# Setting a guard's limit to zero in a fused attention and gating kernel

## The chip, the cores and the metric

The kernel runs on one core of a Trainium2 chip. A core has five engines that run side by side, each through its own list of instructions in order: PE (TensorE, matrix products), DVE (VectorE), ACT (ScalarE), POOL (GpSimd) and SP (SyncE, which here only issues transfers). They meet through semaphores. PE reads SBUF and writes PSUM, which has eight banks of 128 x 512 fp32; a product is a weight load (PEld in the profile) followed by a matmul that streams up to 512 columns.

The metric is the device time of one execution in microseconds (us), lower is better. The time before is 208.46 us, the median of 2 runs (208.24 and 208.68).

## The reference

The input x has 2048 rows of 512 numbers. Two branches are computed from it and mixed row by row. Branch A is a linear attention with 32 heads of 16 channels:

```
qkv = x @ wqkv                               q, k, v: 32 heads of 16
pq = q @ w_phi[h] ; pk = k @ w_phi[h]
phi(p) = concat(softmax(p), softmax(-p))     over the 16 features of a head
kv = sum over rows of phi_k^T v ; z = sum over rows of phi_k
o  = (phi_q @ kv) / (phi_q . z + 1e-6)
a  = o @ wo
```

Branch B is a gated MLP with 1376 hidden channels, split into two halves of 688:

```
z = gelu(x @ w_in) ; z1, z2 = halves of z ; z2 = layernorm(z2)
g = w_sp @ z2 + b_sp                         w_sp mixes the 2048 rows
b = (z1 * g) @ w_out
out = s * a + (1 - s) * b,  s = sigmoid(x . gate_w)
```

## The kernel before

The rows are cut into 16 tiles of 128. The kernel has these stages, and every engine gets its instructions in the order in which the program is written (a manual schedule), so that an instruction that waits holds up everything behind it on its engine.

1. **Loads and z.** A few products with constants (spin, L195) come first on PE, then for each tile z = x @ w_in (L186), gelu on ACT, layer norm statistics on DVE, and v = x @ wv. w_phi is folded into wq and wk (L311), so that pq and pk each come from four 128 x 512 products (feat_mm, L335).
2. **K with the row mixing.** For each tile, k_proj makes pk in PSUM, ACT takes exp(pk) and exp(-pk) from it (feat_exp, L343) into a slot of 1024 bf16 numbers, and k_norm divides by the sums: a sum over each group of 16 (L364, DVE), a reciprocal (L365, DVE), and the product, half of it on POOL and half on DVE (both L371). kv_acc adds phi_k^T v of eight groups of heads into PSUM banks 3 and 4 (kv_mm, L407). Between these the products of w_sp with z2 run (gg_half, L435).
3. **Q and the output.** For each tile q_proj and q_norm do the same for q; a transposing DMA on SP's queue turns the slot around (L401). q_mm multiplies it with kv (eight products, L473), q_num divides by the denominators (reciprocal L479 and product L481, both DVE) and sends the result through another transposing DMA on SP's queue (L488). out_tile makes ten 512-column products (six L494, four L499), copies the bank to SBUF on ACT (L508) and sends it to DRAM from ACT's queue.

These exponentials have no maximum subtracted. The kernel therefore keeps a **guard**: in each norm, POOL adds the sums and their reciprocals into a tile called worst, which starts at 1.0 (L180, L367). Near the end check_sums takes each partition's largest entry and writes 1 to safeb where it is at most SAFE, otherwise 0 (L456). count_safe adds the 128 entries of safeb on PE (L461), and set_flag writes 1 to flag if the total is below 127.5 (L466). All engines read that flag into a register (L616), and after the output products of tile 13 (out_mm, into bank 5) they branch on it (L620).

- If the flag is 0, the If block finishes tiles 13, 14 and 15: three copies, the output products of the last two tiles, and the stores.
- If the flag is 1, the Else block computes branch A once more for all 16 tiles, in the **general** form, and writes the whole output again. Here feat_exp_max takes the place of feat_exp: for each sign DVE reduces the 512 numbers of a tile to 32 maxima (or minima) from PSUM, DVE subtracts them into an fp32 buffer, and ACT takes the exponential of that buffer. The norm leaves out the addition to worst. The uT tiles of branch B (the rows z1 * g, transposed) are still in SBUF and are used again.

The PSUM banks of the Else block are 2 and 6 for pk in turn, 5 and 7 for pq, 3 and 4 for kv and for q_mm, and 2 and 6 for the output.

Of the kernel before, what the change touches and what calls it, by code (L numbers as in the profile page):

```python
# [22 lines left out]
NT = S // P  # L23
# [10 lines left out]
QW = HW + 4  # L34
WSLOTS = 8
LAG = 3
SAFE = 1e30


@with_exitstack  # L40
def kernel(
# [285 lines left out]
    def e_slot(i):  # L327
        if i == 5:
            flat = xn[:].rearrange("p t d -> p (t d)")
        else:  # L330
            flat = w_in_flat[:, i * 2 * D:(i + 1) * 2 * D]
        return flat.rearrange("p (g a n) -> p g a n", g=NHG, a=2)
# [27 lines left out]
    def norm(e, watch=True):  # L360
        ev = e.rearrange("p g a (h f) -> p (g a h) f", h=4)
        zr = ring2.tile([P, 2, 2 * H], FP32, name="zr")
        zs, rs = zr[:, 0, :], zr[:, 1, :]
        nc.vector.tensor_reduce(out=zs, in_=ev, axis=AX.X, op=ALU.add)  # L364
        nc.vector.reciprocal(out=rs, in_=zs)  # L365
        if watch:
            nc.gpsimd.tensor_tensor(  # L367
                out=worst[:], in0=worst[:], in1=zr[:].rearrange("p a h -> p (a h)"), op=ALU.add
            )
        for eng, sl in ((nc.gpsimd, slice(H, 2 * H)), (nc.vector, slice(0, H))):  # L370
            eng.tensor_tensor(  # L371
                out=ev[:, sl, :], in0=ev[:, sl, :],
                in1=rs[:, sl, None].to_broadcast([P, H, DH]), op=ALU.mult,
            )

    def feat(t, w, b, e, general):
        for dt in range(NDT):
            feat_mm(t, w, b, dt)
        if general:
            feat_exp_max(b, e, t)  # L380
        else:
            feat_exp(b, e)

    def k_proj(t, general=False):
        ek_t[t] = e_slot(t % 4)
        feat(t, wk, KBANK[t % 2], ek_t[t], general)

    def k_norm(t, watch=True):
        norm(ek_t[t], watch)

    def q_proj(t, general=False):
        eq_t[t] = e_slot(4 + t % 2 if t < 4 else (t - 4) % 6)
        feat(t, wq, QBANK[t % 2], eq_t[t], general)
# [3 lines left out]
    def q_norm(t, watch=True):  # L397
        e = eq_t.pop(t)
        norm(e, watch)
        eT = wqkT[:, 2 * (t % 4):2 * (t % 4) + 2, :].rearrange("p a (b n) -> p (a b) n", n=P)  # L400
        nc.sync.dma_start_transpose(out=eT, in_=e.rearrange("p g a n -> p (g a n)"))  # L401
        eT_t[t] = eT
# [3 lines left out]
    def kv_mm(t, g):  # L406
        nc.tensor.matmul(  # L407
            slots[:, g, 0:HW + 1], lhsT=ek_t[t][:, g, :, :].rearrange("p a n -> p (a n)"),
            rhs=vv[:, t, g, 0:HW + 1],
            start=(t == 0 and g % 4 == 0), stop=(t == NT - 1), skip_group_check=True,  # L410
        )

    def kv_acc(t):
        for g in range(NHG):
            kv_mm(t, g)

    def kv_extract():
        nc.vector.tensor_tensor(
            out=kvx[:, :, 0:HW].rearrange("p g (h d) -> p g h d", h=4),
            in0=slots[:, :, 0:HW].rearrange("p g (h d) -> p g h d", h=4),  # L420
            in1=mask4[:, None, :, None].to_broadcast([P, NHG, 4, DH]), op=ALU.mult,
        )
        nc.vector.scalar_tensor_tensor(
            out=kvx[:, :, HW:QW], in0=slots[:, :, HW:HW + 1].to_broadcast([P, NHG, 4]),
            scalar=0.5 * DEN_EPS, in1=mask4[:, None, :].to_broadcast([P, NHG, 4]),
            op0=ALU.add, op1=ALU.mult,
        )
# [26 lines left out]
    def check_sums():  # L454
        nc.vector.tensor_reduce(out=worst1[:, 0:1], in_=worst[:], axis=AX.X, op=ALU.max)
        nc.vector.tensor_scalar(  # L456
            out=safeb[:], in0=worst1[:, 0:1], scalar1=SAFE, scalar2=None, op0=ALU.is_le
        )
# [13 lines left out]
    def q_mm(t, g):  # L472
        nc.tensor.matmul(  # L473
            slots[:, g, 0:QW], lhsT=eT_t[t][:, g, :], rhs=kvx[:, g, :], start=True, stop=True
        )

    def q_num(t, general=False):
        rd = ring2.tile([P, NHG, 4], FP32, name="rd")
        nc.vector.reciprocal(out=rd[:], in_=slots[:, :, HW:QW])  # L479
        o = ring2.tile([P, D], BF16, name="o")  # L480
        nc.vector.scalar_tensor_tensor(  # L481
            out=o[:].rearrange("p (g h d) -> p g h d", g=NHG, h=4),
            in0=slots[:, :, 0:HW].rearrange("p g (h d) -> p g h d", h=4),
            scalar=gate[:, t:t + 1],
            in1=rd[:, :, :, None].to_broadcast([P, NHG, 4, DH]), op0=ALU.mult, op1=ALU.mult,
        )
        oT = (gTpool if general else oTpool).tile([P, NDT, P], BF16, name="oT")
        nc.sync.dma_start_transpose(out=oT[:, :, :], in_=o[:, :])  # L488
        oT_t[t, general] = oT

    def out_mm(t, b, n0=0, n1=D, general=False):
        uT, oT = uT_t[t], oT_t[t, general]
        for ft in range(NFT):
            nc.tensor.matmul(  # L494
                ps[:, b, n0:n1], lhsT=uT[:, ft, :], rhs=w_out[:, ft, n0:n1],
                start=(ft == 0), stop=False,
            )
        for g in range(NDT):
            nc.tensor.matmul(  # L499
                ps[:, b, n0:n1], lhsT=oT[:, g, :], rhs=wo[:, g, n0:n1],  # L500
                start=False, stop=(g == NDT - 1),
            )

    def out_copy(t, b, ob, copy, dma, n0=0, n1=D):
        if copy is nc.vector:
            nc.vector.tensor_copy(out=ob[:, n0:n1], in_=ps[:, b, n0:n1])  # L506
        else:
            nc.scalar.activation(out=ob[:, n0:n1], in_=ps[:, b, n0:n1], func=AF.Copy)  # L508
        dma.dma_start(out=out2[t * P:(t + 1) * P, n0:n1], in_=ob[:, n0:n1])

    def out_buf():
        return ring3.tile([P, D], BF16, name="ob")

    def out_tile(t, general=False):
        b = (2, 6)[t % 2]
        out_mm(t, b, general=general)
        out_copy(t, b, out_buf(), nc.scalar, nc.scalar)

    uTpool = ctx.enter_context(tc.tile_pool(name="uTp", bufs=NT))
    oTpool = ctx.enter_context(tc.tile_pool(name="oTp", bufs=LAG + 2))  # L520
    gTpool = ctx.enter_context(tc.tile_pool(name="gTp", bufs=2))

    VLAG = 5
    spin(24)
# [95 lines left out]
    with tc.If(unsafe < 1, label="general", preferred_fallthrough_block=False) as branch:  # L620
# [6 lines left out]
        out_mm(NT - 1, 1, D - P, D)  # L627
        out_copy(NT - 1, 1, ob, nc.scalar, nc.scalar, D - P, D)
    with branch.Else():
        for t in range(NT):  # L630
            k_proj(t, general=True)
            k_norm(t, watch=False)
            kv_acc(t)
        kv_extract()
        for t in range(NT):
            q_proj(t, general=True)
            q_norm(t, watch=False)
            for g in range(NHG):
                q_mm(t, g)
            q_num(t, general=True)  # L640
            out_tile(t, general=True)
# [1 line left out]
_INS = ['A_x', 'A_wqkv', 'A_w_phi', 'A_wo', 'B_x', 'B_w_in', 'B_w_sp', 'B_b_sp', 'B_w_out', 'gate_w']  # L643
_OUTS = [((1, 2048, 512), 'bfloat16')]
# [25 lines left out]
```

## Time and profile before

The profile is of one execution that took 208.59 us, 0.13 us above the median. Its span, from the first to the last instruction, is 206.8 us; the remaining 1.8 us lie outside it.

| stretch (us of the span) | what runs | PE busy | DVE busy | ACT busy | POOL busy |
|---|---|---|---|---|---|
| 0 to 62 | z, v, folding | 60.84 | 38.07 | 39.25 | 2.33 |
| 62 to 129 | K with row mixing | 66.58 | 56.26 | 20.13 | 36.26 |
| 129 to 199.5 | Q with output, row mixing | 70.03 | 54.81 | 20.79 | 24.82 |
| 199.5 to 206.8 | the If block | 4.31 | 1.94 | 0.28 | 0.00 |

A row of a group view reads: line, engine, operation, what it writes and reads with shapes, how often; then the busy time in us, the mean duration of one in ns, and how long the engine stood idle before them. A row of a timeline reads: start in us, duration in us, engine (with a q behind it for the issuing of a transfer), line, operation, and how many instructions the row takes together. The end of a matmul is modelled and includes its way through the array, so in a dense stream the distance between the starts of two matmuls is shorter than their durations. The profile gives a granted TensorE clock of 1.000 for every stretch.

### The profile page before, as it was taken

How to read it: one execution, taken by the hardware profiler on the slowest of the kernel's cores; microseconds unless marked ns; L12 is line 12 of the kernel's file. 1: busy time of each engine (PE TensorE's matmuls, PEld its weight loads, DVE VectorE, ACT ScalarE, POOL GpSimd, SP SyncE). 2: the span in 40 equal slices, each digit the busy share in tenths (PEclk: the TensorE clock that was granted, in tenths of full speed). 3: DMA queues.
4: the chain of work that ended last, by engine and by line, in shares of the span. 5: the costliest groups of instructions: out<-in, count | busy, mean ns of one | idle time of the engine just before them, and what ended most of it. 6: DMA issues, size and time to landing. Idle time of an engine off the chain costs nothing.

```text
span 206.8 us, 3753 instructions
## 1 busy us (share of the span) xinstructions
PE 201.8 (98%) x1376; PEld 118.3 (57%) x1400; DVE 151.1 (73%) x310; ACT 80.4 (39%) x142; POOL 63.4 (31%) x79
## 2 busy tenths in 40 slices
PE   8999999999999999999999999999999999999994
PEld 7654555554455666566666667666455554555542
DVE  1077758385887888879897996798989779796512
ACT  4266767675684323250514101222534233241110
POOL 4000000000003464636474755053643363433000
PEclk9999999999999999999999999999999999999999
DMA  6999999998000639473778882135575966777452
GB/s 170 305 164 205 191 172 224 185 188 240 0 3 0 139 66 115 102 141 63 147 124 92 157 172 41 38 82 111 121 152 117 162 132 128 90 162 153 95 120 65
DMA packets 90384, 26.56 MB, mean 128 GB/s; under 512 B 84296, under 2 KB 90360, under 8 KB 90360
## 3 DMA queue, kind: packets, MB, share of 16 engines
q1 hardware_dynamic: 87648, 24.13, 62.0%
q10 hardware_dynamic: 2712, 2.13, 4.0%
q8 instruction: 12, 0.20, 0.4%
q14 instruction: 12, 0.10, 0.2%
HBM read 3.44 MB, written 2.10 MB: 27 GB/s over the span
## 4 chain that ended last, share of the span: by engine, by line
PE 97%; issue 1%; DVE 0%; ACT 0%; DVEq 0%
PE ps L435 36%; PE ps L186 18%; PE ps L335 13%; PE ps L494 10%; PE ps L288 7%; PE ps L499 6%; PE ps L473 2%; PE ps L407 2%; PE ps L195 2%; PE ps L311 1%; PE ps L201 0%; DVE ob L506 0%; ACT ob L508 0%; PE ps L215 0%; PE ps L461 0%
## 5 line engine op out<-in xcount | busy, mean ns | idle before, releaser
L435 PE MATMUL ps<-zz,wsp 128*128 128x344 bf16 x512 | 84.1, 309 | 0.1
L367 POOL TENSOR_TENSOR worst<-worst,zr 128x128 f32<-128x128 f32 x32 | 28.6, 894 | 124.5 <-DVE zr L365 113.8
L435 PEld LDWEIGHTS <-wsp 128*128 128x128 bf16 x512 | 49.8, 98 | 27.9
L343 ACT ACTIVATE w_in<-ps 128x512 bf16<-128x512 f32 x56 | 30.1, 596 | 63.4 <-POOL w_in L371 20.8
L186 PE MATMUL ps<-w_in,xT 128*128 128x512 bf16 (+2 forms) x197 | 40.1, 356 | 0.2
L364 DVE TENSOR_REDUCE zr<-w_in 128x64 f32<-128x1024 bf16 x28 | 33.8, 1208 | 0.0
L443 DVE SCALAR_TENSOR_TENSOR u<-ps,bcol,zz 128x344 bf16<-128x344 f32 x32 | 18.4, 574 | 20.0 <-PE ps L473 8.6
L186 PEld LDWEIGHTS <-xT 128*128 128x128 bf16 x200 | 19.6, 100 | 17.6
L371 POOL TENSOR_TENSOR w_in<-w_in,zr 128x512 bf16<-128x512 bf16 x28 | 29.5, 1052 | 0.0
L221 ACT ACTIVATE zz<-ps 128x1376 bf16<-128x1376 f32 (+2 forms) x18 | 21.4, 1191 | 18.7 <-PE ps L186 18.7
L230 DVE BATCH_NORM_STATS2 stats<-zz 128x6 f32<-128x344 bf16 x32 | 14.9, 507 | 12.9 <-ACT zz L221 12.9
L494 PE MATMUL ps<-w_out,uT 128*128 128x512 bf16 (+2 forms) x100 | 23.4, 366 | 0.2
L407 PE MATMUL ps<-vv,w_in 128*128 128x65 bf16 x128 | 21.7, 193 | 0.0
L371 DVE TENSOR_TENSOR w_in<-w_in,zr 128x512 bf16<-128x512 bf16 x28 | 19.4, 692 | 1.0
L508 ACT ACTIVATE ob<-ps 128x512 bf16<-128x512 f32 (+1 forms) x14 | 8.0, 575 | 27.0 <-PE ps L499 18.2
L365 DVE RECIPROCAL zr<-zr 128x64 f32<-128x64 f32 x32 | 17.7, 553 | 1.1
L335 PEld LDWEIGHTS <-xT 128*128 128x128 bf16 x128 | 10.8, 98 | 9.9
L499 PE MATMUL ps<-wo,oT 128*128 128x512 bf16 (+2 forms) x66 | 16.2, 366 | 0.0
L335 PE MATMUL ps<-wk,xT 128*128 128x512 bf16 x57 | 15.7, 379 | 0.3
L335 PE MATMUL ps<-wq,xT 128*128 128x512 bf16 x57 | 15.6, 379 | 0.3
L473 PE MATMUL ps<-kvx,wqkT 128*128 128x68 bf16 x128 | 15.8, 194 | 0.1
L288 PE MATMUL ps<-wv,xT 128*128 128x512 bf16 x61 | 15.5, 379 | 0.2
(64 smaller groups left out, 145.0 us busy)
## 6 DMA issues: line engine op xcount, KB each, us to landing
out_dram<-ob ACTq DMA_DIRECT2D x13, 128.0 KB, 2.6
w_out<-in_B_w_out_dram SPq DMA_DIRECT2D x1, 640.0 KB, 5.4
w_in<-in_B_w_in_dram SPq DMA_DIRECT2D x2, 256.0 KB, 4.3
wv<-in_A_wqkv_dram SPq DMA_DIRECT2D x1, 512.0 KB, 5.2
wo<-in_A_wo_dram SPq DMA_DIRECT2D x1, 512.0 KB, 5.8
w_in<-in_B_w_in_dram SPq DMA_DIRECT2D x1, 352.0 KB, 4.5
w_in<-in_B_w_in_dram ACTq DMA_DIRECT2D x2, 128.0 KB, 3.9
w_in<-in_B_w_in_dram SPq DMA_DIRECT2D x2, 128.0 KB, 3.5
```

The source lines that it names most:

```text
L186: nc.tensor.matmul(zb[:, n0:n1], lhsT=xT[:, dt, t * P:(t + 1) * P], rhs=w_in[:, dt, n0:n1], start=(dt == 0), stop=(dt == NDT - 1),)
L221: nc.scalar.activation(out=zz[:, t, n0:n1], in_=zbank(t)[:, n0:n1], func=AF.Gelu_apprx_tanh)
L288: nc.tensor.matmul(ps[:, b, :], lhsT=xT[:, dt, t * P:(t + 1) * P], rhs=wv[:, dt, :], start=(dt == 0), stop=(dt == NDT - 1),)
L335: nc.tensor.matmul(ps[:, b, :], lhsT=xT[:, dt, t * P:(t + 1) * P], rhs=w[:, dt, :], start=(dt == 0), stop=(dt == NDT - 1),)
L343: nc.scalar.activation(out=e[:, :, a, :], in_=src, func=AF.Exp, scale=sc)
L364: nc.vector.tensor_reduce(out=zs, in_=ev, axis=AX.X, op=ALU.add)
L367: nc.gpsimd.tensor_tensor(out=worst[:], in0=worst[:], in1=zr[:].rearrange("p a h -> p (a h)"), op=ALU.add)
L371: eng.tensor_tensor(out=ev[:, sl, :], in0=ev[:, sl, :], in1=rs[:, sl, None].to_broadcast([P, H, DH]), op=ALU.mult,)
L407: nc.tensor.matmul(slots[:, g, 0:HW + 1], lhsT=ek_t[t][:, g, :, :].rearrange("p a n -> p (a n)"), rhs=vv[:, t, g, 0:HW + 1], start=(t == 0 ...
L435: nc.tensor.matmul(ps[:, b, 0:HF], lhsT=wsp[:, tt % WSLOTS, s, :], rhs=zz[:, s, FH + h * HF:FH + (h + 1) * HF], start=(s == 0), stop=(s == ...
L494: nc.tensor.matmul(ps[:, b, n0:n1], lhsT=uT[:, ft, :], rhs=w_out[:, ft, n0:n1], start=(ft == 0), stop=False,)
L499: nc.tensor.matmul(ps[:, b, n0:n1], lhsT=oT[:, g, :], rhs=wo[:, g, n0:n1], start=False, stop=(g == NDT - 1),)
```

## The change

SAFE becomes 0.0. Every entry of worst is then compared with 0, so that safeb is 1 only where a partition's largest entry is not above 0. The order of the Else block is rewritten so that tiles overlap: k_proj of tile t+1 is issued ahead of the norm and the accumulation of tile t; q_proj runs two tiles ahead, q_norm one tile ahead, and the output of a tile comes one tile later. The pool of transposed results that only this block uses (gTpool) gets three buffers in place of two. Nothing ahead of the branch is edited but the constant, and the If block stays.

```diff
-SAFE = 1e30
+SAFE = 0.0
...
-    gTpool = ctx.enter_context(tc.tile_pool(name="gTp", bufs=2))
+    gTpool = ctx.enter_context(tc.tile_pool(name="gTp", bufs=3))
...
     with branch.Else():
+        k_proj(0, general=True)
         for t in range(NT):
-            k_proj(t, general=True)
+            if t + 1 < NT:
+                k_proj(t + 1, general=True)
             k_norm(t, watch=False)
             kv_acc(t)
+        q_proj(0, general=True)
+        q_proj(1, general=True)
         kv_extract()
+        q_norm(0, watch=False)
         for t in range(NT):
-            q_proj(t, general=True)
-            q_norm(t, watch=False)
+            if t + 2 < NT:
+                q_proj(t + 2, general=True)
+            if t + 1 < NT:
+                q_norm(t + 1, watch=False)
             for g in range(NHG):
                 q_mm(t, g)
             q_num(t, general=True)
-            out_tile(t, general=True)
+            if t >= 1:
+                out_tile(t - 1, general=True)
+        out_tile(NT - 1, general=True)
```

feat_exp_max, which the Else block calls and the If block never does, reads:

```python
for a, (sc, op) in enumerate(((1.0, ALU.max), (-1.0, ALU.min))):
    nc.vector.tensor_reduce(out=top[:], in_=src, axis=AX.X, op=op)   # PSUM, 512 -> 32
    nc.vector.tensor_tensor(out=d, in0=src, in1=top (broadcast), op=ALU.subtract)
    nc.scalar.activation(out=e[:, :, a, :], in_=d, func=AF.Exp, scale=sc)
```

## The prediction, made before the result was known

> **What bounds the kernel now.** I read the page first (busy time, the 40 slices, the chain), then the groups by line for prices, then the timeline for the distances between instructions, and last the stretch around the branch. From the page:
>
> ```profile
> PE 201.8 (98%) x1376; PEld 118.3 (57%) x1400; DVE 151.1 (73%) x310; ACT 80.4 (39%) x142; POOL 63.4 (31%) x79
> ...
> PE 97%; issue 1%; DVE 0%; ACT 0%; DVEq 0%
> ```
>
> PE is the bound, in every stage: 98% busy and 97% of the chain. DVE, ACT and POOL hide beside it. That is of little use for the changed kernel, since the Else block is work that no row of this trace shows as such. Its prices have to be put together from the groups:
>
> ```profile
> L364 DVE TENSOR_REDUCE zr<-w_in 128x64 f32<-128x1024 bf16 x28 | 33.8, 1208 | 0.0
> L367 POOL TENSOR_TENSOR worst<-worst,zr 128x128 f32<-128x128 f32 x32 | 28.6, 894 | 124.5 <-DVE zr L365 113.8
> L371 POOL TENSOR_TENSOR w_in<-w_in,zr 128x512 bf16<-128x512 bf16 x28 | 29.5, 1052 | 0.0
> ```
>
> A sum over 1024 numbers takes 1.21 us, POOL's half of a norm 1.05 us. DVE's distances from start to start stand in its timeline:
>
> ```profile
> 135.92 0.34 DVE L479 RECIPROCAL rd<-ps 128x32 f32<-128x32 f32 x1
> 136.30 0.75 DVE L481 SCALAR_TENSOR_TENSOR o<-ps,st,rd 128x512 bf16<-128x512 f32 x1
> 136.97 1.21 DVE L364 TENSOR_REDUCE zr<-w_in 128x64 f32<-128x1024 bf16 x1
> 138.21 0.55 DVE L365 RECIPROCAL zr<-zr 128x64 f32<-128x64 f32 x1
> 138.80 0.69 DVE L371 TENSOR_TENSOR w_in<-w_in,zr 128x512 bf16<-128x512 bf16 x1
> 139.41 0.57 DVE L443 SCALAR_TENSOR_TENSOR u<-ps,bcol,zz 128x344 bf16<-128x344 f32 x1
> ```
>
> q_num takes 0.38 + 0.67 = 1.05 us of DVE, a norm 1.24 + 0.59 + 0.61 = 2.44. An instruction that needs the one before it starts 0.03 us after its end, one that doesn't 0.08 before it.
>
> **Which block runs.** worst starts at 1.0 and only gains positive terms, so "at most 0" holds in no partition, the count is 0, and 0 is below 127.5: the flag is 1. The constant itself costs nothing (the comparison stays one instruction of 0.16 us), nor do the third buffer and the new order, unless the Else block runs. Removed is the If block's 7.3 us of span, since PE is done with tile 13 at 199.5; everything ahead of it stays.
>
> **The first general tile.** PE leaves tile 13 at 199.5, four products of 512 columns take 1.03, so DVE's first reduction could start at 200.6. Before, PE goes into the If block without a gap (its first product starts at 199.36), so a branch can be free; the dearest neighbour is SP, which issued its last transfer of L488 1.6 us after what it needed. Bounds 0 and 1.6 us, taken 0.4: **201.0**.
>
> **The new work on DVE.** A reduction of 512: the rows of 1024 (1.208) and of 128 (0.276, L455) give 1.04 ns each and 0.675 for 512, with the 0.03 of a dependent successor 0.71. A subtraction from PSUM: the nearest row is L418, 128x512 from PSUM, 0.680, less 0.08 before an independent successor, 0.61 rounded up. Maxima and minima of a tile: 2 x (0.71 + 0.61) = 2.64 us. Bounds for each of the four: 0.574 (L443, 344 columns) and 0.751 (L481), thus 11 us less or 12 more over 32 tiles. ACT's two exponentials (0.60 each) run beside DVE's next step.
>
> A K tile costs DVE 2.64 + 2.44 = 5.08 us, a Q tile 5.08 + 1.05 = 6.13. PE's K products are only 1.03 + 0.42 us, so PE no longer bounds by its work.
>
> **But PE's order makes DVE wait in K.** On PE, k_proj(t+2) stands behind kv_acc(t), which needs norm(t). DVE's next task after norm(t) is the maximum of t+2. So after each norm, DVE waits for POOL's half, then four of the eight accumulations (those of POOL's half), then four products. POOL's half starts together with DVE's. How late is it? The 128 numbers of worst take POOL 0.89, nearly as long as 512 take alone right after (1.05), and the 0.89 always starts 0.11 after DVE's half, which lasts 0.69. I read this as POOL standing still until DVE's half is over: now POOL's half would end 1.05 after DVE's. Without that wait it would be 0.47 (0.15 + 1.05 - 0.04 - 0.69). I take 1.05.
>
> The Trainium skill (SBUF — State Buffer, section "Who interferes with whom") says that a VectorE instruction with two SBUF inputs and a GpSimd instruction that reads SBUF exclude each other, the later one waiting in full. By it 1.05 holds, without it the sum is 13 us lower; the 0.894 beside 1.052 speaks for it.
>
> **PE's rate.** The granted clock reads 1.000 throughout, yet the trace has two rates:
>
> ```profile
> 0.84 2.72 PE L195 MATMUL ps<-const-bfloat16-1.0 128*128 128x128 bf16 x24 [0.84 <-PEq L654]
> ...
> 20.69 0.39 PE L311 MATMUL ps<-wphi,wqkT 128*128 128x128 bf16 x4
> ```
>
> The same 128 columns are 0.105 us apart at the start ((2.72 - 0.31) / 23), after PE had stood idle, and 0.057 later ((0.39 - 0.22) / 3): a factor of 1.84. The low rate lasted from 0.84 to about 4.6, some 3.8 us of nearly unbroken work. After that PE never rests, so whether a pause brings the low rate back isn't shown. In K, PE would work 1.5 us (2.7 at the low rate) and rest over 5. Such a burst is shorter than the 3.8 us and follows a rest, like the start: I take the low rate in K.
>
> The Trainium skill (TensorE: Matmul & The Clock Gate, "Part 1: The HAM clock gate") states half the clock after an idle window of some 3.4 us, and the full clock again after as long a busy one. The start agrees (3.8 us, 1.84); for the rest no row here does. By it the sum is the 454 below, without it 436.
>
> The wait after a norm is then 1.05 + 0.1 (to PE) + 0.45 (accumulations) + 1.03 x 1.84 = 1.9 + 0.1 (to DVE) = **3.6 us**; at the full rate 1.05 + 0.1 + 0.25 + 1.03 + 0.1 = 2.5. It comes 15 times: ahead of the maxima of tiles 2 to 15 and of the first Q tile. K: 16 x 5.08 + 15 x 3.6 = 135.3, to 336.3.
>
> **Q.** Two maxima, kv_extract (0.68 + 0.18) and norm(0): 5.28 + 0.86 + 2.44 = 8.6, to 344.9. Then the period. DVE alone gives 6.13. A loop over two tiles, from the start of the maximum of t+2: norm(t+1) done at 5.08, POOL and the issue on SP 6.2, the transposing DMA 2.8 (page: 2.7 to 4.9) 9.0, q_mm 9.5, ten output products 11.7, q_proj(t+4), which PE has behind them, 12.8, and DVE starts at 12.9: 6.45 each. SP takes this DMA and that of L488 1.3 apart, so the latter lands near 10.3, before the last four products need it (10.8). At PE's low rate the same loop takes 9.0 + 0.8 + 4.0 + 1.9 + 0.1 = 15.8, or 7.9 each. But here a burst of PE at the low rate lasts 6.7 us, longer than the 3.8 in which the rate rose at the start, and the pauses are near 2.8. I take 6.6, close to the full rate: 13 x 6.6 = 85.8, to 430.7.
>
> **The end.** The last full turn of DVE 6.1, norm(15) 2.44, POOL and issue 1.15, DMA 2.8, q_mm 0.42, q_num 1.15, DMA 2.8, four products 1.03, copy 0.7, store 3.5 (2.6 to land and 0.9 behind it, as at the end before): 22.1, to **452.8**. With the 1.8 us outside the span 454.6; the profiled run is 0.13 above the median, so I say **454 us**.
>
> **Rivals.**
> - PE keeps its full rate. 15 x 1.1 and 13 x 0.15 less: 436 us. The granted clock of 1.000 speaks for it, the first 24 products against it. Chance 0.22.
> - PE is at its low rate in Q too: 13 x 1.3 = 17 more, 471 us. Chance 0.15.
> - DVE never waits, because the products of the next tile are there in time: 15 x 3.6 and 13 x 0.47 less, 394 us. PE's order as written speaks against it. 0.04.
> - The other side, **not slower**: the flag stays 0, the If block runs as before, 208.5 us. It decides at the comparison of L456: one entry of at most 0 as the maximum in all 128 partitions would do, but sums of exponentials and their reciprocals are positive, and worst starts at 1. 0.01.
> - A price above my bounds (fp32 operands on DVE or POOL, a slow fetch of the Else block): over 476. 0.08.
>
> **How the numbers follow.** The forecast has the remaining 0.50; its own range is 440 to 466, from the prices on DVE and from POOL's wait. The range that takes in the neighbours on both sides is 428 to 476; outside lie the last three rivals, 0.13, and the tails of the others. Slower by over 2% 0.99, within 2% 0.01 (2% is about what a measurement of this kernel can tell from no change), faster 0.
>
> **What would show it.** The page after has DVE at some 330 us busy (151 and 180) and PE below 70% of its span, with maxima and subtractions at 64 each near 0.68 us. In K the maximum waits 3.6 us for PE's L335 in every tile, at a period of 8.7; a distance of 0.40 between those four products, not 0.22, shows the low rate. POOL's half starts to last 1.7 where it overlaps DVE's. In Q the period is 6.6. The prediction is wrong if the K period is 7.6 or less, if a subtraction takes 1 us, or if a long gap stands at 199.5.

## The result and the profile after

The changed kernel takes 456.84 us (median of 456.69 and 456.99) against 208.46 before: 2.190 times as long, with a 95% interval of 2.186 to 2.195. The prediction was 454 us in a range of 428 to 476. The profiled execution took 456.99 us, with a span of 455.3.

The page after, lines that answer to those shown of before (busy time of each engine; the granted TensorE clock in 40 slices; the chain of work that ended last; three groups by line, with busy us, mean ns, and idle time before them):

```profile
PE 311.6 (68%) x1914; PEld 159.6 (35%) x1914; DVE 326.7 (72%) x565; ACT 129.7 (28%) x221; POOL 109.9 (24%) x111
...
PEclk9999999999999999995555555555555788779859
...
DVE 9%; PE 8%; DMA 6%; POOL 3%; issue 2%; ACT 0%; POOLq 0%
...
L371 POOL TENSOR_TENSOR w_in<-w_in,zr 128x512 bf16<-128x512 bf16 x56 | 70.3, 1255 | 186.0 <-DVE zr L365 162.3
...
L349 DVE TENSOR_REDUCE top<-ps 128x32 f32<-128x512 f32 x64 | 43.8, 684 | 64.9 <-PE ps L335 64.9
...
L351 DVE TENSOR_TENSOR zz<-ps,top 128x512 f32<-128x512 f32 x64 | 44.3, 692 | 2.2
```

The Else block runs: maxima (L349) and subtractions (L351) are there, 64 of each. The 68 and 72% of the whole span mix two parts: up to 199.5 us PE is busy for 198.4 as before; behind that, in 255.8 us, DVE is busy for 177.7 (69%) and PE for 113.2 (44%), so there no engine is full. The row of L349 says who waits: DVE stood idle for 64.9 us in front of its maxima, all of it for the products of L335. By the timeline 4.0 of these lie in front of the block's first maximum, 46.7 in K (15 waits of 3.12) and 14.2 in Q. PE's granted clock falls to half in the nineteenth of the 40 slices (by the trace's clock records at 206.1 us, 5 us behind PE's first eight products of the block).

Where the 248.5 us of span came from (455.3 less 206.8), read from the starts of L349 in DVE's timeline, beside the prediction's terms:

| stretch | predicted | measured |
|---|---|---|
| first maximum of the Else block at | 201.0 | 200.08 |
| K, to the first maximum of Q | 135.3 | 129.49 |
| into Q, to the maximum of tile 2 | 8.6 | 8.44 |
| 13 Q tiles | 85.8 (6.6 each) | 94.66 (7.28 each) |
| from the maximum of tile 15 to the end | 22.1 | 22.63 |
| span | 452.8 | 455.3 |

K was 5.8 us shorter than forecast and Q 8.9 longer; with the smaller differences in the other rows 2.5 us of the span were left. The two large errors have opposite signs, so the closeness of the total is partly luck.

One K tile of the changed kernel, from the timeline (start, duration, engine, what; in brackets the idle time before it and what ended it):

```profile
211.02 0.69 DVE L349 TENSOR_REDUCE top<-ps 128x32 f32<-128x512 f32 x1 [3.12 <-PE ps L335]
...
215.51 0.69 DVE L371 TENSOR_TENSOR w_in<-w_in,zr 128x512 bf16<-128x512 bf16 x1
215.61 1.51 POOL L371 TENSOR_TENSOR w_in<-w_in,zr 128x512 bf16<-128x512 bf16 x1 [6.79 <-DVE zr L365]
...
217.17 0.40 PE L407 MATMUL ps<-vv,w_in 128*128 128x65 bf16 x4 [0.45 <-POOL w_in L371]
...
217.38 1.90 PE L335 MATMUL ps<-wk,xT 128*128 128x512 bf16 x4
...
219.31 0.69 DVE L349 TENSOR_REDUCE top<-ps 128x32 f32<-128x512 f32 x1 [3.12 <-PE ps L335]
```

DVE's half of the norm ends at 216.20, POOL's at 217.12, then come the four accumulations that need it, then the four products (1.90 us, not the 1.03 they took before), and only at 219.31 DVE's next maximum. The period is 8.29 us, and 3.12 of it are DVE's wait.

### The profile page after: what moved, and what is told of

It is laid out like the page before. It is cut to its first block, busy times and chain, and to the rows that moved or that the text cites. A ratio compares the mean times of both kernels' runs of the same rounds, so it can differ in the third digit from the quotient of the medians.

```text
span 455.3 us, 5445 instructions
## 1 busy us (share of the span) xinstructions
PE 311.6 (68%) x1914; PEld 159.6 (35%) x1914; DVE 326.7 (72%) x565; ACT 129.7 (28%) x221; POOL 109.9 (24%) x111
## 5 line engine op out<-in xcount | busy, mean ns | idle before, releaser
L371 POOL TENSOR_TENSOR w_in<-w_in,zr 128x512 bf16<-128x512 bf16 x56 | 70.3, 1255 | 186.0 <-DVE zr L365 162.3
L349 DVE TENSOR_REDUCE top<-ps 128x32 f32<-128x512 f32 x64 | 43.8, 684 | 64.9 <-PE ps L335 64.9
L355 ACT ACTIVATE w_in<-zz 128x512 bf16<-128x512 f32 x56 | 35.1, 629 | 152.5 <-DVE zz L351 145.9
L364 DVE TENSOR_REDUCE zr<-w_in 128x64 f32<-128x1024 bf16 x56 | 67.7, 1208 | 0.0
L407 PEld LDWEIGHTS <-w_in 128*128 128x128 bf16 x256 | 19.9, 109 | 106.8 <-issue 96.3
L473 PE MATMUL ps<-kvx,wqkT 128*128 128x68 bf16 x256 | 24.5, 209 | 47.0 <-DMA wqkT<-w_in 32.5
L494 PE MATMUL ps<-w_out,uT 128*128 128x512 bf16 x180 | 53.9, 445 | 0.0
L351 DVE TENSOR_TENSOR zz<-ps,top 128x512 f32<-128x512 f32 x64 | 44.3, 692 | 2.2
L335 PE MATMUL ps<-wk,xT 128*128 128x512 bf16 x128 | 44.7, 489 | 0.0
L335 PE MATMUL ps<-wq,xT 128*128 128x512 bf16 x128 | 37.2, 421 | 1.1 <-DVE zz L351 1.1
L473 PEld LDWEIGHTS <-wqkT 128*128 128x128 bf16 x256 | 16.1, 106 | 58.1 <-DMA wqkT<-w_in 40.8
L335 PEld LDWEIGHTS <-xT 128*128 128x128 bf16 x256 | 25.8, 112 | 30.4 <-issue 15.1
L499 PE MATMUL ps<-wo,oT 128*128 128x512 bf16 x120 | 34.8, 417 | 0.3 <-DMA oT<-o 0.3
```

The costliest lines, as they stand in the source:

```text
L335: nc.tensor.matmul(ps[:, b, :], lhsT=xT[:, dt, t * P:(t + 1) * P], rhs=w[:, dt, :], start=(dt == 0), stop=(dt == NDT - 1),)
L349: nc.vector.tensor_reduce(out=top[:], in_=src, axis=AX.X, op=op)
L351: nc.vector.tensor_tensor(out=d.rearrange("p (h f) -> p h f", f=DH), in0=src, in1=top[:, :, None].to_broadcast([P, H, DH]), op=ALU.subtract,)
L371: eng.tensor_tensor(out=ev[:, sl, :], in0=ev[:, sl, :], in1=rs[:, sl, None].to_broadcast([P, H, DH]), op=ALU.mult,)
L407: nc.tensor.matmul(slots[:, g, 0:HW + 1], lhsT=ek_t[t][:, g, :, :].rearrange("p a n -> p (a n)"), rhs=vv[:, t, g, 0:HW + 1], start=(t == 0 ...
L473: nc.tensor.matmul(slots[:, g, 0:QW], lhsT=eT_t[t][:, g, :], rhs=kvx[:, g, :], start=True, stop=True)
```

## The experiments

Times of single executions stand beside 456.84; where there are several, it is said.

### The order alone, and the limit alone

The first kernel is the changed one with the old limit.

```diff
-SAFE = 0.0
+SAFE = 1e30
```

> The new order and the third buffer alone, with the limit back at 1e30. My theory: the Else block isn't entered, and what stands in it costs nothing: 208.5 us, between 207.5 and 209.5. Rival: code that is only fetched or the larger pool costs something of its own: above 212.7.

Measured: 208.41 us (8 runs), 0.9996 times the kernel before, interval 0.996 to 1.003. The new order and the third buffer cost nothing where the Else block isn't entered. The whole slowdown hangs on the constant.

The second is the kernel before with only the constant changed, so that the Else block runs in its old order.

```diff
-SAFE = 1e30
+SAFE = 0.0
```

> The limit at zero alone, with the Else block in its old order. My theory: each Q tile runs through its whole chain by itself (products, maxima, exponentials, norm, transposing DMA, q_mm, q_num, second DMA, output): about 18.6 us a tile; a K tile gains only the 0.8 us in which DVE waits for the exponentials: 9.1 us. Sum 200 + 146 + 298 + 5, about 650 us, between 620 and 680. Rival: the order in which PE takes its work serialises the tiles in the new kernel just as much, so that the old one is within 10% of it: below 503.

Measured: 622.92 us. K takes 9.21 us a tile. Q takes 16.4 and 17.8 in turn, less than the 18.6 expected. They differ because PE's rate rises late in every second tile: the four L499 take 1.04 us in one tile and 1.89 in the tile before. Why both are below 18.6 stays open. Two lines of its timeline show PE in one Q tile, idle until the first transposing DMA has landed and then until the second has:

```profile
493.44 0.63 PE L473 MATMUL ps<-kvx,wqkT 128*128 128x68 bf16 x8 [10.09 <-DMA wqkT<-w_in]
...
497.82 1.04 PE L499 MATMUL ps<-wo,oT 128*128 128x512 bf16 x4 [1.19 <-DMA oT<-o]
```

So the two edits stand against each other in a way that a single comparison with the kernel before can't show: the constant alone adds 414 us, and the new order takes 166 of them back, some 150 of these in Q (K gains 0.92 us a tile).

### Products ahead in K

The products of K tile t+2 go ahead of the accumulation of tile t in PE's order; feat_mm and feat_exp_max are called by themselves for that. DVE's order stays as it was.

```diff
-        k_proj(0, general=True)
+        k_mms(0); k_mms(1); k_max(0)
         for t in range(NT):
             if t + 1 < NT:
-                k_proj(t + 1, general=True)
+                k_max(t + 1)
+            if t + 2 < NT:
+                k_mms(t + 2)
             k_norm(t, watch=False)
             kv_acc(t)
```

> In K of the Else block, the four products of tile t+2 are put ahead of the accumulation of tile t on PE; DVE's order stays. My theory: DVE waits 3.1 us per K tile only because of PE's order. Then DVE runs through: the K period falls from 8.29 to 5.1 us, 14 times 3.2 are saved, about 412 us, between 407 and 418. Rival: the wait is PE's low rate or POOL's slow half, in whatever order; then the period stays above 7 us and the time above 435.

Measured: 412.05 us, 44.8 less. The K period is 5.09 us from tile to tile. Its timeline between two K tiles (the products of the next maximum, DVE's half of the norm, that maximum):

```profile
239.99 1.90 PE L335 MATMUL ps<-wk,xT 128*128 128x512 bf16 x4
...
243.21 0.69 DVE L371 TENSOR_TENSOR w_in<-w_in,zr 128x512 bf16<-128x512 bf16 x1
243.82 0.68 DVE L349 TENSOR_REDUCE top<-ps 128x32 f32<-128x512 f32 x1
```

The products are done 1.9 us before DVE wants them, and the wait is gone, though POOL's half (1.47 us) and PE's low rate (1.90) are both still there. So PE's order is what puts these two on DVE's path; they set how long the wait is, as the next kernels show.

### Filling PE's rests

The four products lasted 1.90 us in place of 1.03. To see whether PE's rest does that, products that nobody reads fill it in the next three kernels.

```diff
             if t + 1 < NT:
                 k_proj(t + 1, general=True)
+            fill(18)      # 128x512 products into the unused bank 0
             k_norm(t, watch=False)
             kv_acc(t)
```

> The new kernel with 18 products of 512 columns into an unused bank, whose results nobody reads, on PE between k_proj of tile t+1 and the accumulation of tile t. My theory: PE's rate falls because PE rests over 5 us per K tile; with the rest filled, the four products are 0.22 us apart and not 0.43, the wait of DVE falls from 3.12 to 2.2, the K period from 8.29 to 7.4: 15 times 0.87 less, about 444 us, between 440 and 448. Rival: the distance of 0.43 comes from something else (the weight loads, a semaphore): the period stays 8.29 and the time 457, or it grows by what the products take.

Measured: 443.77 us, 13.1 less. Its timeline around one K maximum:

```profile
268.10 1.02 PE L335 MATMUL ps<-wk,xT 128*128 128x512 bf16 x4
268.96 4.05 PE L632 MATMUL ps<-wo,const-bfloat16-1.0 128*128 128x512 bf16 x18
269.16 0.69 DVE L349 TENSOR_REDUCE top<-ps 128x32 f32<-128x512 f32 x1 [2.17 <-PE ps L335]
```

The products take 1.02 us again, DVE's wait is 2.17, and the period 7.35. In three of the tiles it is 7.6; around the end of each of these the granted clock is at half for 3.4 us. More work on PE makes the kernel faster, because PE's rate depends on how busy it is. The windows view of the two kernels' K stage (length, then busy time and count of PE, PEld, DVE, ACT and POOL, then the granted clock, DMA share and GB/s), the changed kernel first:

```profile
199.50:332.00 132.50, 41.17 (x199) 15.16 (x198) 82.93 (x116) 20.76 (x33) 23.64 (x16) 0.52 0.00 0
```

```profile
199.50:317.00 117.50, 89.84 (x481) 39.34 (x480) 80.55 (x112) 20.14 (x32) 23.66 (x16) 0.96 0.00 0
```

The granted clock is 0.52 against 0.96. The next kernel fills Q as well: the same `fill(18)` in K, and `fill(8)` ahead of q_mm of every Q tile.

> As the kernel with filling products in K, and 8 more of them in Q, ahead of q_mm of each tile. My theory: in Q too the low rate after PE's rests makes the difference between the 7.28 us measured per tile and the 6.45 of the loop at the full rate. With the rests filled, Q runs at 6.45 to 6.6: 13 times 0.7 to 0.8 less, some 10 us below the kernel that fills K alone, about 433 us, between 428 and 438. Rival: the transposing DMAs set the Q period; then it stays at 7.2 or above, and the time within 3 us of the kernel that fills K alone.

Measured: 444.58 us, no better than K alone. By the total my theory fell; the timeline says otherwise. The first ten Q tiles take 6.58 us each, against 7.29 in the kernel that fills K alone. The gain was then lost in three places: two K periods at 8.29, two rests of PE in Q (2.23 and 2.77 us) after which the low rate came back (tiles of 8.9 and 8.4 us), and the end, 25.3 us from the maximum of tile 15 in place of 21.2, where filling products, partly at the low rate, stand in front of the last q_mm. To separate this, the last of the three fills Q only, and not its end.

```diff
+            if 1 <= t < 13:
+                fill(12)
             for g in range(NHG):
                 q_mm(t, g)
```

> The new kernel with 12 products into an unused bank ahead of q_mm of each Q tile from 1 to 12, none in K and none for the last tiles. My theory: filling both stages gained 0.4 us per Q tile and lost it again at the ends (two long K periods, and the last tiles waiting behind filling products at the low rate). With Q alone filled and the end left free, Q runs at 6.5 to 6.7 us a tile in place of 7.28: 8 to 10 less, about 448 us, between 445 and 452. Rival: the transposing DMAs set Q's period, so nothing is gained: 455 or more.

Measured: 450.21 us, 6.6 less. Q takes 6.64 us a tile over its 13 periods, at a granted clock of 0.95 (0.78 in the changed kernel). So filling the rests is worth 0.64 of the 7.28 us net of the time that the filling products take on PE themselves. DVE's own work of 6.14 is below both.

### POOL's half

In the Else block DVE's half of the multiplication is left out.

```diff
-        for eng, sl in ((nc.gpsimd, slice(H, 2 * H)), (nc.vector, slice(0, H))):
+        halves = ((nc.gpsimd, slice(H, 2 * H)), (nc.vector, slice(0, H)))
+        for eng, sl in halves if watch else halves[:1]:
```

> The new kernel, but in the Else block DVE's half of each norm's multiplication is left out, so half of the features there stay undivided; POOL's half stays. My theory: POOL's half lasts 1.47 us, not 1.05, because it stands still until DVE's half is over. Without that half it lasts 1.05 from 0.13 after the reciprocal, the accumulation can start 0.42 earlier, and the K period falls from 8.29 to 7.87; in all some 6 us less in K and 4 to 10 in Q, 441 to 447 us. Rival: POOL's half is longer here for a reason of its own; then it stays above 1.4 us, and the K period at 8.2 or above.

Measured: 443.01 us, a K period of 7.87. The timeline of this kernel:

```profile
270.06 0.55 DVE L365 RECIPROCAL zr<-zr 128x64 f32<-128x64 f32 x1
270.79 1.05 POOL L372 TENSOR_TENSOR w_in<-w_in,zr 128x512 bf16<-128x512 bf16 x1 [6.82 <-DVE zr L365]
```

The same half takes 1.05 us alone and 1.47 in most tiles (1.41 to 1.51) beside DVE's half. The 0.42 us are lost to DVE's instruction. The Trainium skill (SBUF — State Buffer, section "Who interferes with whom") has the later of two such instructions wait until the first is over. That agrees in kind; by the recorded times 0.55 of DVE's half was still to run when POOL's started (265.41 against 265.27 + 0.69 in one tile of the changed kernel), and POOL lost 0.42 of it.

### Products ahead in both stages

To the kernel with K's products ahead, the same is done for Q: q_mms(0) and q_mms(1) take the free places in the last two K tiles, and q_mms(t + 3) stands right behind the maxima of tile t+2.

```diff
             if t + 2 < NT:
-                q_proj(t + 2, general=True)
+                q_max(t + 2)
+            if t + 3 < NT:
+                q_mms(t + 3)
             if t + 1 < NT:
                 q_norm(t + 1, watch=False)
```

> The products run ahead on PE in K and in Q: those of K tile t+2 (at the end of K, of the first Q tiles) ahead of the accumulation of tile t, those of Q tile t+3 ahead of q_mm and the output of the tiles before. DVE's order stays. My theory: DVE then waits for no product in either stage: K 5.1 us a tile, Q 6.15 to 6.5; against the new kernel 15 x 3.2 and 13 x 0.8 to 1.1 less, 394 to 399 us. Rival: in Q PE's low rate (6.9 us of work a tile) or the DMAs take over as the bound; then Q stays at 7 us or more, and the time above 403.

Measured: 394.73 us (4 runs, 393.75 to 395.32), 1.895 times the kernel before (1.892 to 1.899), 62 us below the changed kernel. One Q tile of DVE's timeline, complete:

```profile
326.59 0.68 DVE L349 TENSOR_REDUCE top<-ps 128x32 f32<-128x512 f32 x1
327.30 0.69 DVE L351 TENSOR_TENSOR zz<-ps,top 128x512 f32<-128x512 f32 x1
327.91 0.68 DVE L349 TENSOR_REDUCE top<-ps 128x32 f32<-128x512 f32 x1
328.62 0.69 DVE L351 TENSOR_TENSOR zz<-ps,top 128x512 f32<-128x512 f32 x1
329.23 1.21 DVE L364 TENSOR_REDUCE zr<-w_in 128x64 f32<-128x1024 bf16 x1
330.47 0.55 DVE L365 RECIPROCAL zr<-zr 128x64 f32<-128x64 f32 x1
331.06 0.69 DVE L371 TENSOR_TENSOR w_in<-w_in,zr 128x512 bf16<-128x512 bf16 x1
331.67 0.35 DVE L479 RECIPROCAL rd<-ps 128x32 f32<-128x32 f32 x1
332.05 0.75 DVE L481 SCALAR_TENSOR_TENSOR o<-ps,st,rd 128x512 bf16<-128x512 f32 x1
332.72 0.68 DVE L349 TENSOR_REDUCE top<-ps 128x32 f32<-128x512 f32 x1
```

There is no wait in it: 6.13 us from maximum to maximum, and 5.09 in K. These are the 6.13 and 5.08 that the prediction added up from rows of the kernel before for DVE's own work. The transposing DMAs and the rate of PE, whose granted clock is still 0.52 in K and 0.80 in Q, are now hidden.

If DVE is the bound, work taken from DVE must show. In the next kernel POOL does both halves of the multiplication in the Else block, with the products still ahead.

```diff
-        for eng, sl in ((nc.gpsimd, slice(H, 2 * H)), (nc.vector, slice(0, H))):
+        for eng, sl in ((nc.gpsimd, slice(H, 2 * H)), (nc.vector if watch else nc.gpsimd, slice(0, H))):
```

> As the kernel whose products run ahead in K and Q, and in the Else block POOL does both halves of each norm's multiplication, DVE none. My theory: with the products ahead DVE's own work is all that is left as the bound (measured 5.09 and 6.14 us a tile), so 0.61 less on DVE is 0.61 less per K tile: 4.48. In Q the chain behind the norm gets longer by POOL's second half (2.1 us, then the transposing DMA 3.1 and q_mm 0.6 must be through before q_num of that tile), which gives 5.75 and not 5.53 a tile. In all about 379 us, between 375 and 384. Rival: DVE isn't the bound, but POOL's half behind it; then the K period doesn't fall below 5.09 and the time is 395 or more.

Measured: 384.77 us (4 runs, 384.65 to 386.21), 1.847 times the kernel before (1.840 to 1.853): 10 us better, but 6 above the 379 expected and just outside its bounds. K takes 4.37 and 4.74 in turn, Q 6.01 on average. The view of waits, for DVE alone, names what is left, first of K, then of Q (engine and line, what it waited for, us in total, times, longest):

```profile
DVE top L349 <- PE ps L335: 6.7, 8, 4.0
```

```profile
DVE rd L479 <- PE ps L473: 7.3, 9, 1.7
```

Of the 6.7 us, 4.0 lie in front of the block's first maximum; K itself has seven waits of 0.3 to 0.7 us, one in every second tile. There the products wait again behind an accumulation, which now needs 2.07 us of POOL. In Q the denominators wait for q_mm behind POOL and the DMA, as expected but by more. This is the fastest kernel here that takes the Else block. Nothing tried takes that block and comes near 208 us: as it stands its DVE work alone is 81 + 98 us (16 tiles of 5.09 and of 6.14) on top of 200.

### Two buffers

```diff
-    gTpool = ctx.enter_context(tc.tile_pool(name="gTp", bufs=3))
+    gTpool = ctx.enter_context(tc.tile_pool(name="gTp", bufs=2))
```

> The new kernel with two buffers for the transposed results in place of three. My theory: the transfer into a buffer comes more than 5 us after the last product that reads its content two tiles before, so the third buffer is worth nothing: 457 us, within 2. Rival: SP's queue holds the transfer back for it, and Q's transposing DMA behind: above 460.

Measured: 455.76 us. The third buffer gains nothing. The 1.1 us less lie in Q (7.19 a tile), where the tiles' periods vary from pair to pair; with one execution nothing is made of them.

## Why the prediction was right, and where it wasn't

**Which block runs: right.** The limit of zero sends every run into the Else block; with the old limit the same code takes 208.41 us.

**The branch: right, and cheaper than taken.** PE goes from tile 13's products to the first K products without a gap:

```profile
198.16 1.03 PE L499 MATMUL ps<-wo,oT 128*128 128x512 bf16 x4
...
199.02 1.89 PE L335 MATMUL ps<-wk,xT 128*128 128x512 bf16 x8
```

The 0.4 us put in for it weren't needed, and the stage before ended 0.3 us earlier in this execution.

**DVE's work: right.** Maxima 0.684 (forecast 0.675), subtractions 0.692 (0.680), and 5.09 and 6.14 us a tile where nothing else bounds. Reading the distances of starts, and not the durations, is what made this exact: the durations of a K tile add up to 5.21.

**DVE's wait in K: the mechanism right, the size too large.** The wait is 3.12 us, not 3.6, and moving the products ahead of the accumulation removes it. Its terms: POOL's half ends 0.92 after DVE's, forecast 1.05; the two handovers and the accumulations in front of the products take 0.29 (217.12 to 217.38, and 0.03 to DVE), forecast 0.65; the products 1.90, as forecast. The term that was mis-sized most is that 0.65, which was put together from rounded tenths. In the sum a wait counts from start to start: 8.29 less 5.09, thus 3.20 us, 0.08 more than the idle time, because the next maximum could start 0.08 before the end of DVE's half. The 0.40 by which 3.6 is above that make 6 us over 15 waits, which is what K came out short.

**PE's low rate in K: right, from a start that was misread.** The rows of the first microseconds were the right neighbours, and the granted clock of 1.000 for them was the misleading one; in the Else block the page does show it, 0.52. But at the start the low rate lasted 5.8 us and not 3.8. The row behind the last one that the prediction counted shows it:

```profile
4.63 2.88 PE L186 MATMUL ps<-w_in,xT 128*128 128x256 bf16 x16
```

At the later rate, 0.057 for 128 columns, sixteen products of 256 columns are 1.8 us of work. In the trace their starts lie 0.213 us apart up to 6.55 us and 0.110 from there on, and its first record of the clock begins at 6.61. K's bursts of 2.7 us are below either figure, so the choice for K holds. Filling the rests gives 0.96 and 7.35 us a tile (7.4 expected), so the rate is worth 0.94 of the 8.29. The Trainium skill (TensorE: Matmul & The Clock Gate, "Part 1: The HAM clock gate") names half the clock after an idle window of some 3.4 us. Here PE rests 5.4 us at a stretch per K tile, and 1.90 over 1.02 is a factor of 1.86: so far the trace agrees. Shorter rests did it too, though. With the products ahead in K the clock fell at 203.9 us, after a single rest of 1.97, and then stayed at 0.52 through all of K, where PE rests 2.16 and 0.45 us a tile. There the measurement decides: no idle window of 3.4 us was needed. Nor does the start agree in the way that the prediction read it, with its 3.8 us; the last section has what fits both.

**Q's period: wrong.** The step that failed is "I take 6.6, close to the full rate", and in it the argument that a burst of 6.7 us lifts the rate and that pauses of 2.8 us keep it. PE's timeline of the changed kernel, q_mm (L473) of seven tiles with the rest before each, and one pair of tiles in more detail:

```profile
377.14 0.64 PE L473 MATMUL ps<-kvx,wqkT 128*128 128x68 bf16 x8 [4.76 <-DMA wqkT<-w_in]
...
383.50 0.43 PE L473 MATMUL ps<-kvx,wqkT 128*128 128x68 bf16 x8 [1.46 <-DVE zz L351]
...
391.50 0.63 PE L473 MATMUL ps<-kvx,wqkT 128*128 128x68 bf16 x8 [4.54 <-DMA wqkT<-w_in]
...
394.48 1.91 PE L499 MATMUL ps<-wo,oT 128*128 128x512 bf16 x4
396.19 1.55 PE L335 MATMUL ps<-wq,xT 128*128 128x512 bf16 x4
397.64 0.43 PE L473 MATMUL ps<-kvx,wqkT 128*128 128x68 bf16 x8
...
399.20 1.03 PE L499 MATMUL ps<-wo,oT 128*128 128x512 bf16 x4
400.06 1.03 PE L335 MATMUL ps<-wq,xT 128*128 128x512 bf16 x4
406.72 0.63 PE L473 MATMUL ps<-kvx,wqkT 128*128 128x68 bf16 x8 [5.63 <-DMA wqkT<-xn]
...
413.31 0.43 PE L473 MATMUL ps<-kvx,wqkT 128*128 128x68 bf16 x8 [1.13 <-DMA wqkT<-w_in]
...
421.63 0.64 PE L473 MATMUL ps<-kvx,wqkT 128*128 128x68 bf16 x8 [4.83 <-DMA wqkT<-w_in]
```

PE takes two tiles close together and then rests for 4.3 to 5.6 us; between the two it rests for 0.9 to 1.7, or not at all, as in the pair shown in detail, one burst of 9.6 us. That isn't twice 2.8. The first tile of a pair starts at the low rate and is late; by then the transposed slot of the second is there or nearly there, and that one runs at the full rate. After the long rest the rate is low again. The loop over two tiles that the prediction wrote down is real, as the chain of work shows (start, duration, what):

```profile
388.20 3.25 DMA wqkT<-w_in
...
391.50 0.63 PE ps L473 x8
392.13 2.56 PE ps L494 x6
394.69 1.71 PE ps L499 x4
396.40 1.36 PE ps L335 x4
...
397.78 0.70 DVE top L349
```

From the maximum at 382.08 to that at 397.78 it is 15.7 us, close to the 15.8 given for the low rate. But the pairs vary (13 periods make 94.66, so 14.6 a pair), because the rate rises at different points of a pair (4.3 us behind the start of q_mm at 362.18, 5.7 behind that at 391.50). With the rests filled Q takes 6.64, near the 6.6 taken and 0.2 above the loop's 6.45 at the full rate. Two things were missed. A loop over two tiles on one engine may run them close together, so that one pause takes nearly all the idle time. And a pause of 2.8 us is no safe one: in the kernel that fills both stages the rate was lost around rests of 2.23 and 2.77 us, while in the one that fills Q alone it outlived a rest of 3.08.

**The rivals.** PE at its full rate throughout, 436 us: no; even the kernel with both stages filled stays at 444.58, with the rests named above. Its price was about right all the same: the gains of filling K alone and Q alone, 13.1 and 6.6 us, would together come to 437, if they add up. PE at the low rate in Q too, 471: half true, in the first tile of every pair. DVE never waits, 394: not in this kernel, but as soon as the products run ahead, and then at 394.73. Not slower: no.

**The end and the sum.** 22.6 against 22.1. The terms that failed, 5.8 us in K and 8.9 in Q, were inside the bounds given and cancel in part.

## What to carry to other kernels

A block that a guard normally skips has no row in the trace; its price can still be added up from neighbours if one adds distances between starts and follows each engine's list of instructions. Where a producer stands behind a consumer of the tile before in one engine's order, the other engine waits for both, whatever the loops are called: moving the producers ahead gave 62 of 457 us here. And an engine that has little to do is not always cheap: PE, busy for less than half of the time in this block, worked at half its rate for most of it, and where that was on the path, products that nobody reads made the kernel faster.

## What the runs showed of the hardware

- PE's low rate returns in the middle of a kernel. With rests of some 5 us per tile the four 512-column products took 1.90 us in place of 1.02 (granted clock 0.52); with the rest filled down to 1.5 and 0.5 us, 1.02 (0.96). At the very start of the span the products are at the low rate as well, for 5.8 us, while the granted clock reads 1.000.
- What sorts the cases is how busy PE was in a window of 3.41 us, and not the length of one rest. In the clock records of the ten runs that take the Else block, changes of the rate lie whole multiples of 3.41 us apart. On that grid, behind 190 us, windows at the full rate kept it 200 times, with PE busy for 40% or more of the window (by its recorded times), and lost it 78 times, with PE busy for 45% or less. At the low rate, 81 windows brought the full rate back, with PE busy for 77% or more, and 351 did not, with 77% or less. At the start of the kernel before, the first window that is full of work ends at 6.61 us, where the rate rises.
- A POOL multiplication of 512 bf16 numbers took 1.41 to 1.51 us beside a DVE multiplication with two operands in SBUF, and 1.05 alone; DVE's own took 0.69 beside it.
- The branch to the other block, hinted ahead of time, showed no gap on PE (199.02 follows the last product of tile 13 at the stream's usual distance).
